# Attention and a mixture of experts on one core: when eight side jobs load, compute and store the sums of w2

## The chip, the cores and the metric

The kernel runs on 1 core of a Trainium2 chip. The metric is the device time of one execution in microseconds (us); lower is better. Below, PE is the matmul engine, DVE the vector engine, ACT the scalar engine, POOL the GpSimd engine, and SP the engine whose queue issues most of the DMAs.

## The reference

Per batch and head, attention over 576 positions goes through 32 memory slots. The result x (4608 rows of 512) then goes through four experts, each a two-layer perceptron with a hidden width of 1024, weighted by `p`:

```
a = softmax(phi, axis=2);  k_m = einsum('bhsm,bhsd->bhmd', a, k);  v_m = likewise with v
attn = softmax(q @ k_m.T / 8);  x = attn @ v_m          # (8, 8, 576, 64) -> (4608, 512)
p = domain_probs / sum(domain_probs)
for e in range(4):
    h = maximum(x @ w1[e], 0)                            # 4608 x 1024
    out += p[:, e:e+1] * (h @ w2[e])
```

All matmuls carry a value as two parts, a rounded high part and the remainder ("low"), and take three products (high by high, high by low, low by high). So every operand has to be split before it is used: ACT copies the high part, and DVE or POOL subtracts it (`split`, lines 156 and 157).

## The kernel before, in words

**Stages and steps.** The batches go in four pairs. The first two pairs take 2 x 128 = 256 numbered steps (`PAIR` = 128 steps for a pair, 32 for an expert: two batches, two row halves, eight blocks `j` of the hidden width). In step s the order of the program is: `accumulate` (L702, the results of a finished expert pass; for the last expert also the store L705), then `run_plan(s)`, then `first(s + 2)`, then `second(s)`. `first` makes the hidden activations of step s + 2 on PE (L647 to L649), ACT writes their high part (L659) and DVE their low part (L661, tile `h`). `second` multiplies them with w2 (L680 to L682; L682 is the product that needs the low part). PE therefore runs about two steps behind DVE. From step 36 on, nothing is rescheduled: each engine works through its own queue in just this order, so an instruction that waits holds up all that stands behind it on its engine. The two later pairs (`unit`, L1008 and others) use a scheme of products that needs sums of blocks of w2.

**The plan.** All side work hangs on steps, by tables of numbers written by hand: `at(s, unit)` puts a unit into step s, and `run_plan(s)` emits what was put there, in the order of putting. The units that matter here:

- Eight jobs `sums(s, own, e, fh)` (lines 195 to 238), one for each expert `e` and half `fh`, in the order of `JOBS`. A job loads two raw tiles of w2 on SP (L208, 512 KB each), makes four in-place sums on DVE (L231 to L234, two per step), then four times copies a high part on ACT (L220) and subtracts it on POOL (L221), and stores the results to memory by four DMAs that POOL issues (L226, 512 KB each). With `own` true its raw tiles lie in the one buffer `a` and the high parts in `tl` and `ph`, buffers that the attention of later batches uses as well; otherwise they take a buffer of `AT` (three) and two of `kvs` (three). So the next job with `own` can load only after the last one's stores have landed.
- `four` (lines 575 to 618): for the steps that use it, POOL splits a raw w1 tile in step s (L157), PE multiplies it in step s + 2 (L585, first with the high part, then with the low), ACT and DVE write the result into a `kvs` buffer (`vst`, L590 and L591), and POOL issues its store one step later (L573). These run from steps 70 and 230 on, one split in each step.
- `load_w2` (L193) and `load_vw` (L624) on SP fetch weights back, eight DMAs in a group; the program gives SP's DMAs eight landing semaphores in turn, so each of them waits until the one eight places ahead has landed.
- `units_w2` (L157 on POOL) splits w2 tiles in steps 61 to 68 and 93 to 100; `keep_w2` (L184 on POOL) stores split tiles.

The later pairs read the stored sums only from line 856 on, long after the jobs.

Of the kernel before, what the change touches and what calls it, by code (L numbers as in the profile page):

```python
# [28 lines left out]
PAIR = E * STEPS  # L29
# [40 lines left out]
UNITS = (NG - SEVEN) * E * 2 * 4  # L70
Q = 256
X_BANK, Y_BANK, AB_BANK = 4, 2, 6
JOBS = (62, 87, 99, 108, 117, PAIR + 28, PAIR + 85, PAIR + 94)
KEEP_AT, W2_AGAIN = 20, 24
FOUR_AT_7 = ((0, 4, 8, 12), (16, 20, 24, 28))
VW_LOAD_7 = ((21, 37), (26, 41))
# [4 lines left out]
def body(ctx: ExitStack, tc: tile.TileContext, qm, qt, kv, kvt, phi, prob, w1, w1d, w2, out):  # L81
# [105 lines left out]
    def keep_w2(e, j):  # L187
        leave(("w2", e, j), w2t[0, e, j])
        leave_now()
# [6 lines left out]
    def sums(s, own, e, fh):  # L196

        kept = []
        top, low = slice(0, Q), slice(Q, DM)
        sub, v = nc.vector.tensor_sub, nc.vector  # L200

        def load():
            tag = {"tag": "a"} if own else {"tag": "AT", "bufs": 3}
            t = att.tile([P, 2, 2, DM], F32R, name="raw", **tag)
            kept.extend(t[:, i].bitcast(F32) for i in range(2))
            kept.append(t)
            for i in range(2):
                nc.sync.dma_start(kept[i], w2[e, 2 * fh + i])  # L208

        def high(i, j):  # L210
            if j == 0:
                if own and i:
                    t = att.tile([P, 2, 640], F32R, name="sv", tag="ph")
                    t = t.rearrange("p a c -> p (a c)")[:, :2 * DM].rearrange("p (a c) -> p a c", a=2)
                elif own:
                    t = att.tile([P, 2, DM], F32R, name="sv", tag="tl")
                else:
                    t = att.tile([P, 2, DM], F32R, name="sv", tag="kvs", bufs=KVS)
                kept.append(t)
            nc.scalar.copy(kept[3 + i][:, j], kept[i][:, j])  # L220
            nc.gpsimd.tensor_sub(kept[2][:, i, j], kept[i][:, j], kept[3 + i][:, j].bitcast(F32))  # L221

        def store(i):
            d = dram.tile([P, 2, 2, DM], F32, name=f"v{e}{fh}{i}")
            for r, src in enumerate((kept[3 + i], kept[2][:, i])):
                nc.gpsimd.dma_start(d[:, :, r], src.bitcast(F32))  # L226
            for j in range(2):
                kept_for["v", e, fh, 2 * i + j] = d[:, j]

        at(s, load)  # L230
        at(s + 3, lambda: v.tensor_add(kept[1][:, :, low], kept[0][:, :, low], kept[1][:, :, low]))  # L231
        at(s + 3, lambda: sub(kept[0][:, :, low], kept[0][:, :, top], kept[0][:, :, low]))
        at(s + 4, lambda: sub(kept[0][:, :, top], kept[1][:, :, low], kept[0][:, :, top]))
        at(s + 4, lambda: sub(kept[1][:, :, top], kept[1][:, :, top], kept[0][:, :, top]))  # L234
        for i in range(2):
            for j in range(2):
                at(s + 4 + 2 * i + j, lambda i=i, j=j: high(i, j))
            at(s + 6 + 2 * i, lambda i=i: store(i))

    def units_w1(e, fh, g):  # L240
        kept = []
# [468 lines left out]
    def at(s, unit):  # L710
        plan[s].append(unit if isinstance(unit, tuple) else (None, unit))
# [76 lines left out]
    for k in range(NG):  # L788
        for e in range(E):
            s = k * PAIR + e * STEPS  # L790
# [34 lines left out]
    for e in range(E):  # L825
        for j in range(NJ):
            at(e * STEPS + KEEP_AT + j, lambda a=(e, j): keep_w2(*a))
    for n, s in enumerate(JOBS):
        sums(s, s != PAIR + 28, n // 2, n % 2)
    for s in FIRST_LOADS:  # L830
        at(s, lambda: load_part(wp.tile([P, 2, DM], F32R, name="w2", tag="w2", bufs=NJ + 1)))

# [447 lines left out]
```

## Time and profile before

| what | value |
|---|---|
| three timed runs | 1411.23, 1411.86, 1415.82 us; median 1411.86 |
| the profiled execution | 1409.54 us, its span 1407.4 us |
| granted PE clock | 0.994 on average |
| DMA over the span | 301.37 MB, 214 GB/s |
| loads of the jobs (L208) | 16, from 234.1 to 708.7 us, 3.8 to 12.0 us to land |
| stores of the jobs (L226) | 32, from 256.0 to 728.2 us |

The profile comes from one execution. Its times count from the first instruction. A line of it names an engine, a line of the kernel, what is written and read, and in brackets the idle time of that engine just before, with what ended it. A step is dated by the first L680 of its `second`: steps 72, 122, 227 and 230 begin at 262.40, 407.27, 708.34 and 727.20 us.

### The profile page before, as it was taken

Reading aid. Unit: us, or ns where it says so; the run is one execution under the profiler, and the core shown is the slowest. Engines: PE = TensorE matmul, PEld = TensorE weight load, DVE = VectorE, ACT = ScalarE, POOL = GpSimd, SP = SyncE. Lnnn points to the kernel's source line nnn. Section 1 sums busy time; section 2 is a strip of 40 time slices with the busy share of each in tenths; the row PEclk is TensorE's granted clock in tenths of the full one; section 3 lists DMA queues with packets and bytes.
Section 4 is the critical chain, followed back from the end, with each engine's and each line's share of the span. In section 5 each row is a group of like instructions: output and inputs, shape, how many; then the busy total and the mean of one; then the engine's idle time right before and its main releaser. Section 6 shows DMA issues by size and latency. Waiting matters only on the chain.

```text
span 1407.4 us, 25235 instructions
## 1 busy us (share of the span) xinstructions
PE 1366.8 (97%) x8894; PEld 1250.2 (89%) x8894; DVE 837.9 (60%) x1894; ACT 624.8 (44%) x1536; POOL 621.4 (44%) x660
## 2 busy tenths in 40 slices
PE   7899999999999999999979999999999999999998
PEld 6688888888878888889868999899999999999998
DVE  7775545446754365354434467777667666666665
ACT  7654555433444364463225354555543333333332
POOL 4410344755552334422245276676763334333333
PEclk9999999999999999999989999999999999999999
DMA  7832327799684264444588898999985776666662
GB/s 252 272 104 84 123 85 246 228 354 318 226 313 163 90 226 145 139 140 124 188 272 292 278 311 289 314 315 331 321 306 154 223 190 179 177 180 177 178 177 80
DMA packets 102029, 301.37 MB, mean 214 GB/s; under 512 B 24976, under 2 KB 26128, under 8 KB 101904
## 3 DMA queue, kind: packets, MB, share of 16 engines
q1 hardware_dynamic: 81168, 224.26, 51.3%
q0 software_dynamic: 20736, 75.51, 13.8%
q8 instruction: 71, 1.16, 0.4%
q14 instruction: 54, 0.44, 0.1%
HBM read 213.46 MB, written 84.93 MB: 212 GB/s over the span
## 4 chain that ended last, share of the span: by engine, by line
PE 58%; DMA 1%; DVE 1%; ACT 0%; issue 0%; POOL 0%; SPq 0%; DVEq 0%; ACTq 0%
PE banks L1008 22%; PE banks L922 5%; PE banks L923 5%; PE banks L924 5%; PE banks L682 3%; PE banks L680 3%; PE banks L681 3%; PE banks L585 2%; PE banks L647 2%; PE banks L648 2%; PE banks L649 2%; PE banks L1046 1%; PE banks L1047 1%; PE banks L1048 1%; PE banks L469 1%; PE banks L363 1%
## 5 line engine op out<-in xcount | busy, mean ns | idle before, releaser
L1026 DVE SCALAR_TENSOR_TENSOR acc<-banks,pt,acc 128x256 f32<-128x256 f32 x416 | 200.0, 481 | 108.9 <-PE banks L1008 105.2
L157 POOL TENSOR_TENSOR w<-stage,w 128x512 fp32r<-128x512 f32 x134 | 176.6, 1323 | 166.0 <-ACT w L156 153.9
L682 PE MATMUL banks<-w,h 128*128 128x512 f32 x512 | 201.9, 395 | 14.3 <-DVE h L661 14.3
L661 DVE SCALAR_TENSOR_TENSOR h<-banks,h 128x256 fp32r<-128x256 f32 x256 | 107.6, 420 | 164.3 <-ACT h L659 101.6
L680 PE MATMUL banks<-w,h 128*128 128x512 f32 x512 | 202.2, 395 | 1.7 <-DVE acc L702 1.3
L681 PE MATMUL banks<-w,h 128*128 128x512 f32 x512 | 201.7, 394 | 0.0
L659 ACT ACTIVATE h<-banks 128x256 fp32r<-128x256 f32 x256 | 97.8, 384 | 193.1 <-PE banks L649 152.2
L647 PE MATMUL banks<-AT,vw 128*128 128x256 f32 (+1 forms) x512 | 157.4, 308 | 5.7 <-ACT kvs L351 2.2
L1008 PE MATMUL banks<-w,a 128*128 128x256 f32 x1080 | 154.6, 282 | 0.3 <-DVE acc L1026 0.2
L648 PE MATMUL banks<-AT,vw 128*128 128x256 f32 (+1 forms) x512 | 151.7, 297 | 0.0
L922 PE MATMUL banks<-AT,vw 128*128 128x256 f32 (+1 forms) x512 | 151.6, 296 | 0.0
L649 PE MATMUL banks<-AT,vw 128*128 128x256 f32 (+1 forms) x512 | 151.2, 296 | 0.1
L923 PE MATMUL banks<-AT,vw 128*128 128x256 f32 (+1 forms) x512 | 151.1, 295 | 0.0
L924 PE MATMUL banks<-AT,vw 128*128 128x256 f32 (+1 forms) x512 | 150.9, 295 | 0.0
L1008 PEld LDWEIGHTS banks<-w,a 128*128 128x128 f32 x1080 | 143.6, 188 | 4.9 <-issue 0.9
L989 POOL TENSOR_TENSOR vt<-ph,vt 128x512 fp32r<-128x512 f32 x64 | 84.1, 1314 | 107.3 <-ACT vt L988 78.3
L682 PEld LDWEIGHTS banks<-w,h 128*128 128x128 f32 x512 | 96.5, 189 | 37.4 <-DVE h L661 16.0
L352 POOL TENSOR_TENSOR kvs<-stage,kvs 128x512 fp32r<-128x512 f32 x58 | 75.8, 1325 | 101.4 <-ACT kvs L351 100.9
L647 PEld LDWEIGHTS banks<-AT,vw 128*128 128x128 f32 x512 | 97.1, 190 | 18.0 <-DVE vw L562 4.0
L680 PEld LDWEIGHTS banks<-w,h 128*128 128x128 f32 x512 | 96.6, 189 | 13.7 <-DVE acc L702 1.8
L681 PEld LDWEIGHTS banks<-w,h 128*128 128x128 f32 x512 | 96.6, 189 | 11.0
L156 ACT CAST w<-stage 128x512 fp32r<-128x512 f32 x168 | 102.7, 619 | 6.3 <-DMA stage<-in_w 4.1
(149 smaller groups left out, 2985.6 us busy)
## 6 DMA issues: line engine op xcount, KB each, us to landing
w<-kw SPq DMA_DIRECT2D x93, 512.0 KB, 5.3
vwd<-vst POOLq DMA_DIRECT2D x80, 512.0 KB, 6.2
vw<-vwd SPq DMA_DIRECT2D x320, 128.0 KB, 5.7
w<-v SPq DMA_DIRECT2D x55, 512.0 KB, 5.5
stage<-in_w SPq DMA_DIRECT2D x44, 512.0 KB, 4.3
stage<-in_w1d SPq DMA_DIRECT2D x40, 512.0 KB, 4.7
stage<-in_kv SPq DMA_DIRECT2D x32, 512.0 KB, 3.9
kw<-w POOLq DMA_DIRECT2D x32, 512.0 KB, 6.7
```

The source lines that it names most:

```text
L157: eng.tensor_sub(dst[:, 1, :], raw, dst[:, 0, :].bitcast(F32))
L647: nc.tensor.matmul(ps, w[:, 0, f], at_t[:, g, 0, c], start=g == 0, stop=False)
L648: nc.tensor.matmul(ps, w[:, 0, f], at_t[:, g, 1, c], start=False, stop=False)
L649: nc.tensor.matmul(ps, w[:, 1, f], at_t[:, g, 0, c], start=False, stop=g == 1)
L680: nc.tensor.matmul(po[t], x[:, 0, :], w[:, 0, :], start=j == 0, stop=False)
L681: nc.tensor.matmul(po[t], x[:, 0, :], w[:, 1, :], start=False, stop=False)
L682: nc.tensor.matmul(po[t], x[:, 1, :], w[:, 0, :], start=False, stop=j == NJ - 1)
L922: nc.tensor.matmul(ps, w[:, 0, f], at_t[:, g, 0, c], start=g == 0, stop=False)
L923: nc.tensor.matmul(ps, w[:, 0, f], at_t[:, g, 1, c], start=False, stop=False)
L924: nc.tensor.matmul(ps, w[:, 1, f], at_t[:, g, 0, c], start=False, stop=g == 1)
L1008: nc.tensor.matmul(ps, a[:, l, jj], w[:, r, c], start=start and jj + i == 0, stop=jj == 1 and i == 2, skip_group_check=True,)
L1026: VE.scalar_tensor_tensor(a, src, p, a, ALU.mult, ALU.add)
```

## The change

The sums of a job come five and six steps after its load instead of three and four, and the later parts of the job move by the same two steps. The eight jobs start at other steps, and the one after step 128 that uses the shared buffers is joined by the first one. In order of the job:

| job (e, fh) | load before | load after | first sums before | first sums after |
|---|---|---|---|---|
| 1 (0, 0) | 62, own | 60, shared | 65 | 65 |
| 2 (0, 1) | 87 | 62 | 90 | 67 |
| 3 (1, 0) | 99 | 87 | 102 | 92 |
| 4 (1, 1) | 108 | 99 | 111 | 104 |
| 5 (2, 0) | 117 | 111 | 120 | 116 |
| 6 (2, 1) | 156, shared | 152, shared | 159 | 157 |
| 7 (3, 0) | 213 | 213 | 216 | 218 |
| 8 (3, 1) | 222 | 225 | 225 | 230 |

```diff
-JOBS = (62, 87, 99, 108, 117, PAIR + 28, PAIR + 85, PAIR + 94)
+JOBS = (60, 62, 87, 99, 111, PAIR + 24, PAIR + 85, PAIR + 97)
...
-        at(s + 3, lambda: v.tensor_add(kept[1][:, :, low], kept[0][:, :, low], kept[1][:, :, low]))
-        at(s + 3, lambda: sub(kept[0][:, :, low], kept[0][:, :, top], kept[0][:, :, low]))
-        at(s + 4, lambda: sub(kept[0][:, :, top], kept[1][:, :, low], kept[0][:, :, top]))
-        at(s + 4, lambda: sub(kept[1][:, :, top], kept[1][:, :, top], kept[0][:, :, top]))
+        at(s + 5, lambda: v.tensor_add(kept[1][:, :, low], kept[0][:, :, low], kept[1][:, :, low]))
+        at(s + 5, lambda: sub(kept[0][:, :, low], kept[0][:, :, top], kept[0][:, :, low]))
+        at(s + 6, lambda: sub(kept[0][:, :, top], kept[1][:, :, low], kept[0][:, :, top]))
+        at(s + 6, lambda: sub(kept[1][:, :, top], kept[1][:, :, top], kept[0][:, :, top]))
         for i in range(2):
             for j in range(2):
-                at(s + 4 + 2 * i + j, lambda i=i, j=j: high(i, j))
-            at(s + 6 + 2 * i, lambda i=i: store(i))
+                at(s + 6 + 2 * i + j, lambda i=i, j=j: high(i, j))
+            at(s + 8 + 2 * i, lambda i=i: store(i))
...
-        sums(s, s != PAIR + 28, n // 2, n % 2)
+        sums(s, s not in (60, PAIR + 24), n // 2, n % 2)
```

What this does to POOL's queue around steps 68 to 72, before. `raw_2441` and its `sv` tiles are those of job 1, `w2` is a split for the second expert layer, and `w1_2649` and `w1_2672` are the splits for the first two `four` multiplications:

```order
L157 TENSOR_TENSOR w2_2606<-stage_2398,w2_2606 128x512
L226 DMA v000_2609<-sv_2550 256x1x512
L226 DMA v000_2609<-raw_2441 256x1x512
L221 TENSOR_TENSOR raw_2441<-raw_2441,sv_2612 128x512 x2
L157 TENSOR_TENSOR w1_2649<-stage_2459,w1_2649 128x512
L226 DMA v001_2652<-sv_2612 256x1x512
L226 DMA v001_2652<-raw_2441 256x1x512
L157 TENSOR_TENSOR w1_2672<-stage_2459,w1_2672 128x512
```

The same place after. `raw_2383` is job 1, `raw_2444` job 2; the two splits for `four` are now `w1_2661` and `w1_2690`:

```order
L226 DMA v000_2614<-raw_2383 256x1x512
L221 TENSOR_TENSOR raw_2383<-raw_2383,sv_2617 128x512
L221 TENSOR_TENSOR raw_2444<-raw_2444,sv_2622 128x512
L221 TENSOR_TENSOR raw_2383<-raw_2383,sv_2617 128x512
L221 TENSOR_TENSOR raw_2444<-raw_2444,sv_2622 128x512
L157 TENSOR_TENSOR w1_2661<-stage_2462,w1_2661 128x512
L226 DMA v001_2664<-sv_2617 256x1x512
L226 DMA v001_2664<-raw_2383 256x1x512
L226 DMA v010_2667<-sv_2622 256x1x512
L226 DMA v010_2667<-raw_2444 256x1x512
L221 TENSOR_TENSOR raw_2444<-raw_2444,sv_2670 128x512
L157 TENSOR_TENSOR w1_2690<-stage_2462,w1_2690 128x512
```

Two subtractions of job 2 have come ahead of the first split, and two stores and one subtraction more ahead of the second.

SP's queue around the load of job 8 (`raw`), before. `w` is a tile of w2 (512 KB), `vw` a quarter tile (128 KB):

```order
L193 DMA w_6947<-kw_4088 128x1024
L193 DMA w_6967<-kw_4115 128x1024
L208 DMA raw<-in_w 128x1024 x2
L193 DMA w_6987<-kw_4150 128x1024
L624 DMA vw<-vwd_2950 32x1024
L624 DMA vw<-vwd_2980 32x1024
L624 DMA vw<-vwd_3012 32x1024
L624 DMA vw<-vwd_3052 32x1024
```

And after:

```order
L193 DMA w_6981<-kw_4161 128x1024
L624 DMA vw<-vwd_2973 32x1024
L624 DMA vw<-vwd_3003 32x1024
L624 DMA vw<-vwd_3035 32x1024
L624 DMA vw<-vwd_3075 32x1024
L624 DMA vw<-vwd_3109 32x1024
L624 DMA vw<-vwd_3141 32x1024
L624 DMA vw<-vwd_3168 32x1024
L624 DMA vw<-vwd_3201 32x1024
L208 DMA raw<-in_w 128x1024 x2
```

The two raw loads have moved behind one more tile of w2 and a whole group of eight `vw` loads.

## The prediction

> **What bounds the kernel now.** First the busy shares on the page, then PE's table of waits, then the view of the line that makes a job's first sum (L231), for what DVE waited for:
>
> ```profile
> PE 1366.8 (97%) x8894; PEld 1250.2 (89%) x8894; DVE 837.9 (60%) x1894; ACT 624.8 (44%) x1536; POOL 621.4 (44%) x660
> PE banks L682 <- DVE h L661: 14.3, 4, 9.9
>   DMA raw<-in_w: 19.5, 2
> ```
>
> PE is busy for all but 40.6 us of the 1407.4 us span, so the change can only win PE's waits, or add to them. Its largest wait is for the low part `h` of DVE, 14.3 us in 4 times; and DVE itself stood still for 19.5 us in two of the eight jobs because a raw tile had not landed. The timelines of DVE and PE show the two places (start, duration, ..., idle before with its releaser):
>
> ```profile
> 408.20 0.69 DVE L231 TENSOR_TENSOR raw<-raw 128x512 f32<-128x512 f32 x1 [5.55 <-DMA raw<-in_w]
> 410.01 0.50 PE L682 MATMUL banks<-w,h 128*128 128x512 f32 x1 [2.11 <-DVE h L661]
> 717.07 0.69 DVE L231 TENSOR_TENSOR raw<-raw 128x512 f32<-128x512 f32 x1 [13.94 <-DMA raw<-in_w]
> 718.87 0.79 PE L682 MATMUL banks<-w,h 128*128 128x512 f32 x1 [9.90 <-DVE h L661]
> ```
>
> Jobs 5 and 8 hold DVE; PE has about 4 us of lead and waits for the rest, 2.11 and 9.90 us. The second costs more than its gap. PE's timeline dates the steps by their first L680 (steps 226, 227, 228 and 230), and the table by windows has the granted clock (third value from the end):
>
> ```profile
> 706.25 0.40 PE L680 MATMUL banks<-w,h 128*128 128x512 f32 x1
> 708.34 0.40 PE L680 MATMUL banks<-w,h 128*128 128x512 f32 x1
> 722.02 0.63 PE L680 MATMUL banks<-w,h 128*128 128x512 f32 x1
> 727.20 0.40 PE L680 MATMUL banks<-w,h 128*128 128x512 f32 x1
> 712.00:716.00 4.00, 0.00 (x0) 0.00 (x0) 0.00 (x0) 0.00 (x0) 0.00 (x0) 0.69 1.03 412
> 716.00:720.00 4.00, 1.13 (x3) 0.94 (x4) 2.87 (x5) 0.51 (x1) 0.00 (x0) 0.50 1.05 248
> 720.00:724.00 4.00, 4.00 (x15) 3.38 (x14) 1.41 (x4) 2.58 (x7) 3.72 (x5) 0.53 0.65 201
> ```
>
> An undisturbed step takes 708.34 - 706.25 = 2.09 us. Steps 227 to 229 took 727.20 - 708.34 = 18.86 us, so the place costs 18.86 - 3 x 2.09 = 12.6 us: 9.9 of waiting, the rest at a clock of about 0.5. The most that the two waits hold is 2.1 + 12.6 = 14.7 us.
>
> **Job 5 (before at 117, now at 111).** SP's waits and its timeline:
>
> ```profile
> SPq L208 <- DMA v<-raw: 15.8, 2, 10.0
> 398.00 1.69 SPq L208 DMA_DIRECT2D raw<-in_w  x2
> ```
>
> Its load stood on SP until job 4's stores, planned in steps 114 and 116, had landed, which was in step 118 (396.8 to 399.6 us); the tiles came 10 us later, at 408.1. Now the stores are planned in 107 and 109: landed two steps later again, they free the load at its own step 111, and 10 us, under four steps of 2.8, end in step 115, ahead of the sums in 116. I take the whole 2.1 us as won. Should the landing take 3 us more, DVE's 4 us of lead cover it. Jobs 3, 4, 6 and 7 waited for nothing on DVE and get two steps more: nothing, with up to 1.5 us either way for transfers that meet others.
>
> **Job 8 (before at 222, now at 225).** SP's timeline, and two rows of its waits:
>
> ```profile
> 707.12 0.89 SPq L193 DMA_DIRECT2D w<-kw  x2
> 708.24 1.82 SPq L208 DMA_DIRECT2D raw<-in_w  x2
> 710.58 9.53 SPq L624 DMA_DIRECT2D vw<-vwd  x8
> SPq L624 <- DMA w<-kw: 7.0, 5, 2.5
> SPq L624 <- DMA raw<-in_w: 2.0, 2, 1.1
> ```
>
> The DMAs are full here (a share of 1.03 to 1.05 above), and SP runs some four steps behind the plan, each DMA waiting for the landing of an earlier one. So placing the load three steps later doesn't just move it in time: the raw tiles now go behind one `w` and eight `vw`, 0.52 + 1.05 = 1.57 MB. At 412 GB/s that is 3.8 us, at 330 (the mean of the first two windows) 4.8 us, so they land not at 717.0 but at about 721 (719 to 722.5, since job 7's stores, two steps later too, mix in differently). PE would want h of step 232 at 708.34 + 3 x 2.09 + 2 x 2.25 (the wider half, an estimate) + 0.5 = 719.6. From landing to PE took 718.87 - 717.0 = 1.9 us, so PE gets it at 722.9: a wait of 3.3 us is left.
>
> Then comes POOL. Job 8's subtractions now stand between the `four` splits of steps 232 to 236, whereas before they stood ahead of all of these. POOL's pitch is read from this stretch of its timeline, with the two PE rows that use the splits and the next step's L680s:
>
> ```profile
> 250.96 1.30 POOL L221 TENSOR_TENSOR raw<-raw,sv 128x512 fp32r<-128x512 f32 x1 [2.35 <-ACT sv L220]
> 252.21 1.30 POOL L157 TENSOR_TENSOR w<-stage,w 128x512 fp32r<-128x512 f32 x1
> 255.95 0.67 POOL L226 DMA_DIRECT2D v<-sv  x1
> 256.57 0.78 POOL L226 DMA_DIRECT2D v<-raw  x1
> 257.16 2.75 POOL L221 TENSOR_TENSOR raw<-raw,sv 128x512 fp32r<-128x512 f32 x2
> 259.64 1.49 POOL L157 TENSOR_TENSOR w<-stage,w 128x512 fp32r<-128x512 f32 x1
> 262.05 3.02 POOL L157 TENSOR_TENSOR w<-stage,w 128x512 fp32r<-128x512 f32 x2
> 261.19 0.50 PE L585 MATMUL banks<-w,vs 128*128 128x512 f32 x1 [0.86 <-POOL w L157]
> 262.40 0.40 PE L680 MATMUL banks<-w,h 128*128 128x512 f32 x1
> 263.79 0.63 PE L585 MATMUL banks<-w,vs 128*128 128x512 f32 x2
> 265.13 0.40 PE L680 MATMUL banks<-w,h 128*128 128x512 f32 x1
> ```
>
> A subtraction or split takes 1.25 us, a store's issue 0.6. From the sums' end (3.2 us after the landing) to the split of step 236 stand four L221, five L157, four L226 and four L573: 9 x 1.25 + 8 x 0.6 = 16 us. That is 721 + 19.5 = 740.5; PE, at 265.13 - 262.40 = 2.73 us a step with `four`, wants it 1.2 us ahead of step 238, at 719.1 + 6 x 2.73 - 1.2 = 734.3. So some 6.2 us of the 12.6 come back in pieces, and 6.4 us are won (4 to 9 over the landing's range).
>
> **Jobs 1 and 2 (now at 60 and 62).** Job 1's sums stay in step 65, so POOL still starts its first subtraction at 250.96. In the rows above it then never rests, and the first `four` already waits 0.86 us for it. Now two L221 of job 2 come ahead of the first split: 2.5 us. And job 2's sums meet a busy POOL, which before happened only rarely (POOL, DVE, POOL):
>
> ```profile
> 867.66 1.29 POOL L157 TENSOR_TENSOR w<-stage,w 128x512 fp32r<-128x512 f32 x1 [2.04 <-ACT w L156]
> 867.82 1.68 DVE L499 TENSOR_TENSOR at<-at,z 128x512 f32<-128x512 f32 x1
> 868.91 1.74 POOL L989 TENSOR_TENSOR vt<-ph,vt 128x512 fp32r<-128x512 f32 x1
> ```
>
> A DVE operation of two SBUF tiles and a POOL one don't run together: DVE's takes 1.68 instead of 0.69 and POOL's next 1.74 instead of 1.29, 0.45 more. Three such meetings add 1.35. The first split ends at 261.13 + 2.5 + 1.35 = 265.0, and PE is 3.8 us late. [...]
>
> Ahead of the second split stand four stores in a row now. POOL has issued a fourth store of a job only after the first of the four had landed:
>
> ```profile
> 694.91 0.92 POOL L226 DMA_DIRECT2D v<-sv  x1
> 698.12 0.69 POOL L226 DMA_DIRECT2D v<-raw  x1 [2.29 <-issue]
> 426.02 0.69 POOL L226 DMA_DIRECT2D v<-raw  x1 [3.82 <-DMA v<-sv]
> v<-sv POOLq DMA_DIRECT2D x16, 512.0 KB, 4.3
> DMA to landing us min/median/max: 3.0/4.9/11.3
> ```
>
> The first goes at 264.75; landing takes 3.0 at least and 4.3 in the median of v<-sv; the DMAs are not full at 266, so I take 3.5. The fourth is issued at 268.25, the subtraction follows 0.6 later, the split 1.25 after that and lasts 1.5: 271.6. Before, PE used it at 264.02 (the second of the pair at 263.79) without waiting. So PE is 7.6 us late in all. [...] Later splits come at less than a step's work and add nothing. DVE's delayed sums cost PE under 2 us at steps 69 and 70, which this larger wait swallows.
>
> **The sum**, against the profiled execution: 1409.54 - 2.1 - 6.4 + 7.6 = 1408.6. Its time lies 2.3 us below the median of the runs shown, so on the runs' scale that is 1411.0, against 1411.86: no change that a measurement could tell, whose bound is about 0.3%, 4.2 us.
>
> **The rivals.** *Faster.* Job 8's tiles land by 717.7 and POOL gives nothing back (all 12.6 won), and jobs 1 and 2 cost 4.8: -2.1 - 12.6 + 4.8 = -9.9, 1402. For it: SP's queue loses the raws' own 1.05 MB ahead of `vw`. Against it: those bytes only change places in full DMAs. Half of that, 4.2 us, is enough to be seen. I give 0.27 to all such cases.
>
> *Slower.* One mechanism, POOL at jobs 1 and 2: a fourth store that waits for a landing of 8 us instead of 3.5, adding 4.5, and decides from 6.5 us on. PE then idles over 8 us in one piece and the clock falls to 0.5 as at 713, another 2.5 us: 1411.0 + 4.5 + 2.5 = 1418. For it, landings up to 11.3; against it, DMA queues that aren't full there. 0.13. [...]
>
> *The change doesn't do what it says.* Job 8's loads, queued last, land at 725 or later and DVE waits as long as before; 6.4 won becomes 2.5: 1415. 0.1, half of it beyond the bound.
>
> **How the numbers follow.** The forecast, its terms within their bounds, has 0.5, the faster rival 0.27, POOL's 0.13, job 8's 0.1. The low end is near the faster rival, the high end near POOL's: 1403 to 1417.5. Faster by over 0.3%: 0.27. Slower: 0.13 + 0.05 = 0.18. Within: 0.55.
>
> **What would show it.** Right: no wait of DVE for raw near job 5; L585 waiting 6 to 9 us in all for POOL's split near 260 to 272; a fourth L226 there with a gap; DVE waiting for raw at job 8 for 5 to 9 us with PE waiting 2 to 5 behind it, then short waits of L585 for POOL. Wrong: L585 without waits near 262, or job 8's L231 without one.

## The result, and the profile after

Over seven runs each, taken together, the changed kernel takes 1423.30 us in the median (1418.77 to 1426.04) and the kernel before 1412.34 us (1408.67 to 1416.47). The ratio is 1.0069, 95% interval 1.0046 to 1.0093: slower by 11 us between the medians, by 10 by the ratio. The forecast was 1411.0, its range ended at 1417.5.

The profiled execution of the changed kernel took 1425.06 us, its span is 1423.2 us. It lies at the upper end of its runs, and the profiled execution of before (1409.54 us) at the lower end of its own, so the two profiles are further apart than the medians. Its first row on the page, PE's busy time:

```profile
PE 1377.2 (97%) x8894; PEld 1257.0 (88%) x8894; DVE 846.0 (59%) x1894; ACT 625.3 (44%) x1536; POOL 623.4 (44%) x660
```

Of the 15.8 us by which the span has grown, 10.4 are busy time of PE (1366.8 before), with the same 8894 matmuls: more of them ran at half clock (granted clock 0.988 on average, 0.994 before). PE's table of waits after (us in total, times, the longest):

```profile
PE banks L585 <- POOL w L157: 7.2, 4, 3.6
PE banks L682 <- DVE h L661: 7.1, 5, 4.0
...
PE banks L585 <- DVE vst L591: 2.2, 1, 2.2
...
PE banks L680 <- ACT h L659: 2.1, 3, 1.3
...
PE banks L647 <- DVE h L661: 1.9, 1, 1.9
```

The one wait of 9.9 us for `h` is gone. In its place stand six of 1.3 to 4.0 us, for POOL's split, for `h`, for `vst` and for ACT.

Where the time went is read from the steps, dated by their first L680 as before. The table gives, for stretches of steps, how much longer the stretch took than in the profile of before; the last three columns are experiments told below (pair_alone, six_alone and late_alone). Stretches that are not listed differ by 0.1 us at most, except 255 to the end of the span (-0.1 to +1.8; the last section has the reason).

| steps | changed | jobs 1, 2 alone | job 6 alone | jobs 7, 8 alone |
|---|---|---|---|---|
| 0 to 8 | +1.66 | -0.47 | +0.62 | -0.57 |
| 64 to 80 (jobs 1, 2) | **+10.38** | **+9.45** | 0.00 | 0.00 |
| 80 to 104 | -0.65 | -3.15 | -0.56 | -0.88 |
| 120 to 128 (job 5) | **-2.84** | +1.09 | +1.25 | +1.22 |
| 152 to 176 (job 6) | **+4.06** | -0.35 | **+2.75** | -0.44 |
| 224 to 248 (jobs 7, 8) | **+2.26** | -0.12 | +0.77 | **-0.23** |

With the 1.0 us by which step 0 began later, the first column gives the 15.8. The head of the program (up to step 8) is the same in all kernels of this study, and differs by -1.1 to +2.4 us from profile to profile: that is no effect of the change. Steps 80 to 104 are not steady either: the eight kernels of this study that run as before up to step 104 differ from it there by -0.88 to +0.25 us.

**Jobs 1 and 2.** POOL's timeline around the first two splits for `four`, and the two matmuls of PE that wait for them:

```profile
266.12 1.49 POOL L157 TENSOR_TENSOR w<-stage,w 128x512 fp32r<-128x512 f32 x1
267.32 0.94 POOL L226 DMA_DIRECT2D v<-sv  x1
...
268.49 1.21 POOL L226 DMA_DIRECT2D v<-sv  x1
271.04 0.69 POOL L226 DMA_DIRECT2D v<-raw  x1 [1.34 <-issue]
271.62 1.40 POOL L221 TENSOR_TENSOR raw<-raw,sv 128x512 fp32r<-128x512 f32 x1
272.84 1.39 POOL L157 TENSOR_TENSOR w<-stage,w 128x512 fp32r<-128x512 f32 x1
...
267.66 0.50 PE L585 MATMUL banks<-w,vs 128*128 128x512 f32 x1 [3.03 <-POOL w L157]
274.29 0.79 PE L585 MATMUL banks<-w,vs 128*128 128x512 f32 x1 [3.63 <-POOL w L157]
```

The picture is the one that was forecast: POOL rests only ahead of the fourth of four stores in a row, for 1.34 us, and L585 waits 6.66 us in two pieces (0.86 us in all before).

**Job 5.** DVE's first sum starts without a wait, where it waited 5.55 us before:

```profile
403.78 1.09 DVE L231 TENSOR_TENSOR raw<-raw 128x512 f32<-128x512 f32 x1
```

**Job 6.** Two rows of DVE in steps 157 and 158 of the changed kernel (L274 belongs to the softmax of `phi`), ACT's rows behind them, and the two waits of PE that follow:

```profile
517.59 0.15 DVE L274 TENSOR_SCALAR nm<-nm 128x1 f32<-128x1 f32 x1
...
520.89 0.68 DVE L233 TENSOR_TENSOR raw<-raw 128x512 f32<-128x512 f32 x1
...
521.60 0.62 ACT L220 CAST sv<-raw 128x512 fp32r<-128x512 f32 x1 [2.63 <-DVE raw L233]
522.12 0.38 ACT L659 ACTIVATE h<-banks 128x256 fp32r<-128x256 f32 x1
...
527.50 0.50 PE L680 MATMUL banks<-w,h 128*128 128x512 f32 x1 [1.30 <-ACT h L659]
533.28 0.58 PE L647 MATMUL banks<-AT,vw 128*128 128x256 f32 x1 [1.94 <-DVE h L661]
```

The same piece of ACT's work before:

```profile
518.57 0.61 ACT L220 CAST sv<-raw 128x512 fp32r<-128x512 f32 x1
519.09 0.37 ACT L659 ACTIVATE h<-banks 128x256 fp32r<-128x256 f32 x1
```

ACT now stands 2.63 us at its first copy. That copy needs the sum of L233, and DVE reaches its sums only behind its part of the softmax of `phi`. ACT's high part of `h` stands behind the copy in ACT's queue. Before, the copies came after the softmax and ACT did not wait at them.

**Job 8.** The load on SP, the first sum on DVE, PE's wait for `h`, and, 25 us later, a wait of ACT for a `vst` buffer whose store had not landed, with PE's behind it:

```profile
732.04 0.83 SPq L208 DMA_DIRECT2D raw<-in_w  x2
...
737.27 0.69 DVE L231 TENSOR_TENSOR raw<-raw 128x512 f32<-128x512 f32 x1 [10.16 <-DMA raw<-in_w]
739.08 0.79 PE L682 MATMUL banks<-w,h 128*128 128x512 f32 x1 [3.97 <-DVE h L661]
...
763.44 0.59 ACT L590 CAST vst<-banks 128x512 fp32r<-128x512 f32 x1 [5.26 <-DMA vwd<-vst]
764.90 0.77 PE L585 MATMUL banks<-w,vs 128*128 128x512 f32 x1 [2.22 <-DVE vst L591]
```

The table by windows for these places. The windows are those of 3.41 us in which the clock is granted (last section); busy PE stands second, the granted clock third from the end:

```profile
734.18:737.59 3.41, 0.93 (x6) 0.49 (x4) 0.32 (x1) 0.00 (x0) 0.00 (x0) 1.00 0.96 378
737.59:741.00 3.41, 1.92 (x5) 1.53 (x6) 2.94 (x7) 1.17 (x4) 0.38 (x1) 0.50 0.03 13
741.00:744.42 3.42, 3.42 (x12) 2.99 (x11) 3.42 (x8) 3.42 (x10) 3.40 (x4) 0.50 0.42 153
...
764.90:768.31 3.41, 3.13 (x10) 2.42 (x11) 2.16 (x6) 2.50 (x7) 2.78 (x4) 0.50 0.53 215
768.31:771.72 3.41, 3.41 (x11) 2.83 (x10) 2.02 (x5) 0.54 (x3) 2.40 (x4) 0.50 0.69 272
```

At each of the two waits, 3.97 and 2.22 us, the clock is halved for 6.83 us, from inside the first wait and from the end of the second. Before, one wait of 9.90 us had 10.24 us at half clock (713.53 to 723.77 us), and the wait itself lasted until 718.87, through half of them.

### The profile page after: what moved, and what is told of

Read it like the earlier page. It is cut to its first block, busy times and chain, and to the rows that moved or that the text cites. A ratio compares the mean times of both kernels' runs of the same rounds, so it can differ in the third digit from the quotient of the medians.

```text
span 1423.2 us, 25232 instructions
## 1 busy us (share of the span) xinstructions
PE 1377.2 (97%) x8894; PEld 1257.0 (88%) x8894; DVE 846.0 (59%) x1894; ACT 625.3 (44%) x1536; POOL 623.4 (44%) x660
## 4 chain that ended last, share of the span: by engine, by line
PE 84%; DVE 6%; DMA 4%; ACT 2%; issue 2%; POOL 1%; SPq 0%; ACTq 0%; DVEq 0%; POOLq 0%
PE banks L1008 22%; PE banks L682 8%; PE banks L681 8%; PE banks L680 8%; PE banks L922 5%; PE banks L923 5%; PE banks L924 5%; PE banks L647 4%; PE banks L648 4%; PE banks L649 4%; PE banks L585 2%; PE banks L469 2%; PE banks L363 2%; DVE vw L562 1%; PE banks L1046 1%
## 5 line engine op out<-in xcount | busy, mean ns | idle before, releaser
L680 PE MATMUL banks<-w,h 128*128 128x512 f32 x512 | 203.9, 398 | 4.5 <-ACT h L659 2.1
L647 PEld LDWEIGHTS banks<-AT,vw 128*128 128x128 f32 x512 | 98.1, 192 | 19.5 <-DVE vw L562 4.7
L680 PEld LDWEIGHTS banks<-w,h 128*128 128x128 f32 x512 | 97.5, 190 | 17.4 <-ACT h L659 3.6
L648 PEld LDWEIGHTS banks<-AT,vw 128*128 128x128 f32 x512 | 98.4, 192 | 8.6 <-DVE AT L532 0.3
```

What stands on the lines that cost most here:

```text
L647: nc.tensor.matmul(ps, w[:, 0, f], at_t[:, g, 0, c], start=g == 0, stop=False)
L648: nc.tensor.matmul(ps, w[:, 0, f], at_t[:, g, 1, c], start=False, stop=False)
L680: nc.tensor.matmul(po[t], x[:, 0, :], w[:, 0, :], start=j == 0, stop=False)
```

## The experiments

In the edits a job is written as (step of the load, own buffers, steps from the load to the first sums), and where a fourth number stands, it is the steps from the load to the first copy on ACT and its subtraction on POOL (otherwise one more than the third); the stores move with these. All times and ratios are against runs of the kernel before on the same chip.

**pair_alone: jobs 1 and 2 as changed, the rest as before.**

```diff
-JOBS = (62, 87, 99, ...)                      # all three steps
+JOBS = ((60, False, 5), (62, True, 5), (99, True, 3), ...)
```

> Jobs 1 and 2 alone as changed (60 and 62, five steps), jobs 3 to 8 as before. My theory now: the pair costs what the changed kernel shows between steps 64 and 80, 10.4 us: 6.6 us more waiting of PE and some 3.4 us of work at half clock behind the second wait; so the run is 10 us over before and every other place is as before. Rival (the forecast): 7.6 us, the waits alone, and the rest of the 10.4 comes from elsewhere. Rival: the pair is harmless without the later jobs, under 2 us.

Measured: 1417.31 us, ratio 1.0051 (1.0031 to 1.0070), by the ratio 7.2 us over before; steps 64 to 80 take 9.45 us more. So the pair is by far the largest cost, and needs none of the other changes. In steps 80 to 104 it gives 3.15 us back, 1.75 of them in step 99, where before PE waits 1.67 us for a load of q (L469); that wait is gone in all five kernels with job 2 at step 62, a gain that the prediction did not list. At the start of step 73, behind the second split, the profile is 7.69 us late (29.23 us from step 64, against 21.54): just the 7.6 of the forecast (8.66 in the changed kernel, whose clock was halved from 273.38 us, in its second wait). The other 1.8 us come later, by step 80, in which POOL is still catching up (a wait of 0.60 us at L585 in step 77 among them).

**warm: the changed kernel, with 8 matmuls of the identity ahead of each of the first two pairs of L585.**

```diff
-        ps = bank("pm", 512)
+        ps = bank("pm", 512); [nc.tensor.matmul(ps[:, :P], ident, ident, start=True, stop=True) for _ in range(fill.pop(0) if fill else 0)]
```

> The changed kernel with 8 extra matmuls of the identity (result unused) on PE ahead of each of the first two L585 pairs, where PE waits 3.0 and 3.6 us for POOL. My theory: the extra 1.7 us each fit inside the waits, which end when they ended; the clock is not halved at 273 us; the 3.4 us of half speed go, so steps 64 to 80 take 7 us more than before instead of 10.4. Rival: the waits alone made the 10.4; then nothing is won, and up to 1 us is lost.

Measured: 1419.08 us, ratio 1.0062 (1.0040 to 1.0084); steps 64 to 80 take 9.73 us more than before. The windows of the changed kernel at and behind its second wait:

```profile
269.96:273.38 3.42, 0.69 (x4) 0.22 (x2) 0.34 (x2) 0.00 (x0) 2.35 (x3) 1.00 0.94 351
273.38:276.79 3.41, 2.50 (x8) 2.41 (x9) 0.69 (x1) 1.13 (x3) 3.41 (x4) 0.50 0.75 241
276.79:280.20 3.41, 3.41 (x10) 2.64 (x10) 0.56 (x2) 0.54 (x3) 3.41 (x5) 0.50 0.74 275
```

The window of the second wait in warm, and the one behind it:

```profile
268.52:271.94 3.42, 2.46 (x19) 2.07 (x18) 0.31 (x2) 0.00 (x0) 2.36 (x3) 1.00 0.95 353
271.94:275.35 3.41, 2.51 (x13) 2.25 (x14) 1.12 (x3) 1.50 (x4) 3.41 (x4) 1.00 0.74 246
```

The added matmuls kept PE busy for 1.95 us ahead of each pair. The clock did stay whole (1.00 in both windows, against 0.50 in two of the changed kernel), and yet only 0.65 us of the 10.38 went. My theory fell: 6.83 us at half clock cost under 1 us here. POOL sets the pace behind the wait (busy 3.41 of 3.41 us in both), and the faster PE waits for it a little later (0.60 us at L585 in step 77, which the changed kernel has not). What is left is POOL's work, which the next run moves.

**pair_pool_later: pair_alone, with job 2's subtractions and stores behind the `four` splits.**

```diff
-        (62, True, 5)
+        (62, True, 5, 26)
```

> The pair_alone kernel with job 2's subtractions and stores moved on to steps 88 to 92, behind the four splits; its load and its sums stay. My theory: the pair's 9.5 us in steps 64 to 80 are POOL's work ahead of the first four splits; without it they fall under 3 us (job 1's own stands there before the change too, and DVE's sums of two jobs cost some 1.6 us in steps 69 and 70). Rival: the late h of DVE in steps 69 and 70 carries on by itself; then 5 us or more stay.

Measured: 1415.86 us, ratio 1.0029 (1.0016 to 1.0042). Steps 64 to 80 take 1.40 us more than before, instead of 9.45. So job 2's work behind the sums is the cost, and DVE's sums alone are not. ACT's copies moved along with POOL's part in this run; that it is POOL's part shows in the rows above, where PE waits for POOL's splits and POOL hardly rests. PE's row there, and one that came in step 95:

```profile
265.12 0.50 PE L585 MATMUL banks<-w,vs 128*128 128x512 f32 x1 [0.58 <-POOL w L157]
...
336.18 2.31 PE L469 MATMUL banks<-kT,stage 128*128 128x64 f32 x16 [2.89 <-DMA stage<-in_qm]
```

The second row is a wait for a load of q that lasted 0.18 us before; steps 80 to 96 take 2.75 us more with it. Why that load is later here was not tried, and part of the 2.75 may be chance: the changed kernel and six_later (below) are the same program up to step 152, and differ by 2.07 us in steps 80 to 96.

**six_alone: job 6 alone as changed; six_later: the changed kernel with job 6's sums where they stood before.**

```diff
-JOBS = (..., PAIR + 28, ...)                  # six_alone, against before
+JOBS = (..., (PAIR + 24, False, 5), ...)
...
-        (PAIR + 24, False, 5)                 # six_later, against the changed kernel
+        (PAIR + 24, False, 7)
```

> The kernel before with job 6 alone as changed (PAIR + 24, five steps). Theory: job 6's sums in steps 157 and 158 meet the softmax of phi; steps 152 to 176 are 4 us longer than before, as in the changed kernel (0.7 + 4.4 - 1.0), and the run is 3 to 4 us over before. Rival: this needs the other jobs' changes (another phase of SP's queue); then nothing changes.

> The changed kernel with job 6's sums and all behind them two steps later, where they stood before; its load stays at PAIR + 24. My theory: the sums' place against the softmax of phi in steps 157 to 159 costs 3.4 us, so steps 160 to 176 are as before, and the run is 3.4 us under the changed kernel (some 7.5 us over before). Rival: the load's earlier place or chance costs it, and the 3.4 us stay.

Measured: six_alone 1414.34 us, ratio 1.0018 (1.0003 to 1.0032), steps 152 to 176 +2.75 us with the same two waits as in the changed kernel (1.31 and 1.95 us). six_later 1416.18 us, ratio 1.0041 (1.0023 to 1.0060), steps 152 to 176 within 0.14 us of before. The load stayed at its new step there, so it is the place of the sums beside the softmax, and nothing else. The 1.31 us between +4.06 and +2.75 lie in steps 161 and 162, where the clock of the changed kernel was halved for 3.41 us (from 532.79 us) and that of six_alone was not.

**late_alone: jobs 7 and 8 alone as changed.**

```diff
-JOBS = (..., PAIR + 85, PAIR + 94)
+JOBS = (..., (PAIR + 85, True, 5), (PAIR + 97, True, 5))
```

> Jobs 7 and 8 alone as changed (five steps, job 8 at PAIR + 97), jobs 1 to 6 as before. My theory now: steps 224 to 248 take 2 us more than before: PE's wait for h falls from 9.9 to 4 us but is followed by half clock for 6.8 us, and a second wait of some 2 us comes at step 239, where the stores of vst stand behind the four stores of job 8; so the run is within 4 us of before, rather above it. Rival (the forecast): 6.4 us won.

Measured: 1409.22 us, ratio 0.9986 (0.9973 to 0.9998); steps 224 to 248 take 0.23 us less than before. Steps 224 to 232 win 12.43 us, steps 232 to 248 lose 12.20. The rows of PE that lose it, and the row of ACT ahead of the second:

```profile
723.31 0.50 PE L682 MATMUL banks<-w,h 128*128 128x512 f32 x1 [3.67 <-DVE h L661]
...
748.69 0.47 PE L585 MATMUL banks<-w,vs 128*128 128x512 f32 x1 [1.84 <-DVE vst L591]
...
747.23 0.58 ACT L590 CAST vst<-banks 128x512 fp32r<-128x512 f32 x1 [4.74 <-DMA vwd<-vst]
```

Step 232 alone takes 8.42 us instead of 2.73 (5.69 more), steps 235 to 240 take 6.52 more.

**eight_pool_later: late_alone, with job 8's subtractions and stores behind the last `four` split. eight_stores_later: late_alone, with only the stores moved there.**

```diff
-        (PAIR + 97, True, 5)
+        (PAIR + 97, True, 5, 21)              # eight_pool_later
...
-            at(s + hi + 2 + 2 * i, lambda i=i: store(i))
+            at(s + hi + (18 if s == PAIR + 97 else 2) + 2 * i, lambda i=i: store(i))   # eight_stores_later
```

> The late_alone kernel with job 8's subtractions and stores moved on by 15 steps, behind the last four split (from PAIR + 118); its load stays at PAIR + 97 and its sums at PAIR + 102. My theory: the wait of some 3.7 us for the raw tiles at step 232 and its half clock stay (about 6 us with what is lost at half clock), the waits at steps 235 to 239 go: steps 224 to 248 are 6 us shorter than before, against 0.2 in late_alone. Rival: the waits at steps 235 to 239 come from elsewhere (the vst stores themselves, the transfers held up) and stay.

> The late_alone kernel with only job 8's four stores moved on by 16 steps (to PAIR + 121 and PAIR + 123); its subtractions stay between the four splits. In late_alone steps 235 to 240 took 6.5 us more than before. Theory of the stores: the vst stores land late because they stand in POOL's queue behind job 8's 2 MB, and their tiles come free late; then the wait for vst at step 239 goes and steps 235 to 240 are within 2 us of before. Theory of POOL's time (the forecast): the splits are late because of the subtractions; then 4 us or more of the 6.5 stay, and PE waits for the splits.

Measured: eight_pool_later 1405.41 us, ratio 0.9953 (0.9932 to 0.9974); in steps 235 to 240 nothing is lost any more, and in 232 and 233 7.5 us. eight_stores_later 1405.68 us, ratio 0.9948 (0.9932 to 0.9965); steps 235 to 240 lose 1.8 us. All waits of PE from step 232 to 240 in eight_stores_later:

```profile
725.35 0.80 PE L682 MATMUL banks<-w,h 128*128 128x512 f32 x1 [4.02 <-DVE h L661]
742.05 0.50 PE L585 MATMUL banks<-w,vs 128*128 128x512 f32 x1 [0.23 <-POOL w L157]
748.70 0.50 PE L585 MATMUL banks<-w,vs 128*128 128x512 f32 x1 [0.59 <-POOL w L157]
```

No wait for `vst` is left. So of the 6.5 us, 4.7 went with the stores, and 1.8 stay with the subtractions, which stay in place here. How the 4.7 divide between POOL's time in issuing them and the later landing of the `vst` stores behind them in its queue, these runs do not say.

**eight_sums_later: before, with job 8's sums eight steps behind its load.**

```diff
-        (PAIR + 94, True, 3)
+        (PAIR + 94, True, 8)
```

> The kernel before with one thing changed: job 8's sums come eight steps behind its load instead of three (PAIR + 102), with its subtractions and stores behind them as ever. Its load stays at PAIR + 94, so the tiles land at about 717 us. My theory: DVE waits for nothing and the 12.4 us of steps 224 to 232 are won; the subtractions and stores now lie between the four splits and cost PE what steps 235 to 239 of the late_alone kernel show, waits of 3.3 us and half clock worth 1 to 2: steps 224 to 248 are 7 to 8 us shorter than before. Rival: POOL and the stores of vst cost most of the 12 us by themselves; then under 4 us are won.

Measured: 1408.41 us, ratio 0.9970 (0.9957 to 0.9983). Steps 224 to 248 take 6.18 us less than before: 10.17 won up to step 232, 3.99 given back after it. A little less than expected at the front, since PE now waits 0.40 and 1.38 us for a tile of w2 in steps 229 and 231, which the long wait had covered.

**warm_eight: eight_pool_later with 9 matmuls of the identity at the start of step 232.** They stand in `second`, ahead of the first L680, in the same way as in warm.

> The eight_pool_later kernel with 9 extra matmuls of the identity (result overwritten) on PE at the start of step 232, where PE then waits for h because job 8's tiles are late. Theory: the half clock behind this wait costs about 3 us of the 7.5 that steps 232 to 240 lost there; with the extra matmuls the window is busy enough, the clock stays whole, and steps 232 to 240 are 4 to 5 us longer than before instead of 7.5. Rival: as with the pair, another engine sets the pace behind the wait, so the clock makes no difference and the 7.5 stay.

Measured: 1405.88 us, ratio 0.9957 (0.9938 to 0.9976). Steps 224 to 248 take 5.2 us less than before (eight_pool_later 5.0). The matmuls ran in the window ahead of the one that held the rest of the wait (1.19 us of busy PE), and the window behind that one was halved all the same, for 3.41 us instead of the 6.83 of eight_pool_later. So this run does not settle what the clock costs here. The other profiles say a little more: steps 232 to 234 lost 5.6 to 5.8 us where the clock was halved for 3.41 us (eight_stores_later, late_alone, warm), and 6.6 to 7.5 us where it was for 6.83 (six_later, the changed kernel, eight_pool_later). Two of them had almost the same wait, 4.02 us (eight_stores_later) and 3.99 us (six_later), and differ by 1.0 us.

**best: job 5's sums two steps later, job 8's sums and POOL work later. best2: jobs 2 to 5 spaced anew, job 8 loaded later. best3: job 8 alone, loaded later.**

```diff
-JOBS = (62, 87, 99, 108, 117, PAIR + 28, PAIR + 85, PAIR + 94)     # all three steps
+(117, True, 5), (PAIR + 94, True, 8, 24)                            # best: these two
...
+(85, True, 4), (95, True, 4), (105, True, 4), (115, True, 4), (PAIR + 102, True, 13, 16)   # best2: these
...
+(PAIR + 102, True, 13, 16)                                          # best3: this one
```

> The kernel before with job 5's sums two steps later (five behind its load at 117), and job 8 with its load at PAIR + 94 as before, its sums at PAIR + 102 and its subtractions and stores behind the last four split (from PAIR + 118). Jobs 1 to 4, 6 and 7 as before. My theory: job 5 wins 2 to 3 us, job 8 all of its 12.4: 14 us under before, about 1398. Rival: job 8's late stores delay phase two's loads or the opening of its tiles, and 3 us or more come back between steps 246 and 256 or after; or the sums of job 5 in step 122 delay the attention of batch 4.

> Jobs 2 to 5 at 85, 95, 105 and 115 with the sums four steps behind the load (job 1, 6, 7 as before); job 8 loaded at PAIR + 102, its sums at PAIR + 115, its subtractions and stores from PAIR + 118. Theory: job 5's load no longer stands on SP for job 4's stores, so the 2.1 us at step 122 (and half clock) go; job 8's load behind the loads of w and vw ends the waits of 1.1 and 1.7 us for w in steps 229 and 231 that the best kernel has: all 12.4 us of steps 224 to 232 and 2.1 to 3 of steps 120 to 128 are won, 15 us under before in the profile. Rival: the sums in new steps meet the softmax of batches 2 and 3 in steps 92 to 117 and cost 2 us or more there.

> The kernel before with job 8 alone moved: loaded at PAIR + 102, sums at PAIR + 115, subtractions and stores from PAIR + 118. Theory: steps 224 to 248 are 12.4 us shorter than before and nothing else changes; the run is 12 us under before. Rival: the later load meets the loads of vw and the first loads of phase two, and the sums at step 243 come late: 3 us or more are given back between steps 240 and 256.

Measured: best 1403.68 us, ratio 0.9942 (0.9923 to 0.9961). Job 8 wins 9.2 us in steps 224 to 248; job 5 wins nothing (steps 120 to 128 as before). DVE still waits there, since the load stands on SP as long as before:

```profile
410.71 0.69 DVE L231 TENSOR_TENSOR raw<-raw 128x512 f32<-128x512 f32 x1 [3.44 <-DMA raw<-in_w]
```

best2 1407.29 us, ratio 0.9970 (0.9954 to 0.9987). Job 5 is cured (-2.84 us in steps 120 to 128), but steps 80 to 120 take 11.1 us more. PE's largest wait and SP's two rows ahead of it:

```profile
325.33 1.81 SPq L142 DMA_DIRECT2D stage<-in_w  x2
336.76 0.80 SPq L208 DMA_DIRECT2D raw<-in_w  x2
...
348.05 1.11 PE L469 MATMUL banks<-kT,stage 128*64 128x64 f32 x8 [4.13 <-DMA stage<-in_qt]
```

SP's table of waits has what held it:

```profile
SPq L208 <- DMA v<-raw: 21.1, 3, 10.4
```

SP issues nothing from 327 to 337 us, until the stores of the job before have landed, and the load of q stands behind it: steps 99 and 100 lose 5.3 us. (Steps 95 and 96 lose 3.7 more at an earlier load of q, which this hold does not explain.) The softmax met the moved work too, in step 113, where 2.2 us more were lost. Its product on DVE (L499) took 5.11 us instead of 1.22 before, while POOL issued two stores of job 4 and made three operations back to back beside it, and PE waited for the result:

```profile
387.45 5.11 DVE L499 TENSOR_TENSOR at<-at,z 64x256 f32<-64x256 f32 x1
...
393.22 0.34 PE L520 MATMUL banks<-ident,at 64*128 64x64 f32 x2 [1.91 <-DVE AT L532]
```

So the rival held for these 2.2 us, and a larger part, 5.3 us, came through SP.

best3 1399.19 us, ratio 0.9905 (0.9883 to 0.9928): the shortest time here, by the ratio 13 us under before. Its rows of SP and DVE for job 8, and the only wait of PE between steps 224 and 248:

```profile
717.86 0.82 SPq L208 DMA_DIRECT2D raw<-in_w  x2
...
755.80 1.53 DVE L231 TENSOR_TENSOR raw<-raw 128x512 f32<-128x512 f32 x1
...
712.57 0.47 PE L680 MATMUL banks<-w,h 128*128 128x512 f32 x1 [0.91 <-DMA w<-kw]
```

The tiles are loaded when SP has nothing more urgent behind them, the sums come 38 us after the load was issued, and POOL's part lies behind the last `four` split. 11.1 of the 12.6 us that the prediction put on job 8's old place are won.

## Why the prediction was wrong

**Job 5** (forecast -2.1): right, -2.84 in the profile, and for the reason given. Job 4's stores had landed by 386.79 us, the load was issued at 386.94, in its own step 111, and DVE did not wait.

**Jobs 1 and 2** (forecast +7.6): the mechanism was right, step by step, and so was the lateness behind the second split (7.69 us alone). The 1.35 us for three meetings of DVE and POOL held: beside job 2's sums three operations of POOL took 1.74, 1.73 and 1.74 us (from 254.89, 256.59 and 258.27 us), and the one ahead of them 1.29. In the profile of before, DVE's sums and L499 at 128x512 took 0.89 to 1.68 us in the six cases in which an operation of POOL was running at their start, and 0.67 to 0.69 in all others. The landing taken as 3.5 us was 3.4. As for the DMAs at 266 us, which the prediction calls not full: their share in the changed kernel was 0.39 (266.55 to 269.96 us), in before 1.05 (266 to 270). The step "Later splits come at less than a step's work and add nothing" failed: 1.8 us were added by step 80, while POOL was still behind, and 0.9 more in the changed kernel, whose clock was halved there.

**Job 8** (forecast -6.4, measured +2.26, alone -0.23): the wait of PE for `h` was forecast at 3.3 us and measured at 3.67 to 4.38. That it came so near is partly luck, since both its ends were later than forecast: counted from the start of step 227, the tiles landed after 15.3 us in the changed kernel and 13.8 in late_alone (12.7 forecast), and PE came to its wait after 13.2 and 12.1 (11.3 forecast). The step that failed is "some 6.2 us of the 12.6 come back": 12.2 came back in late_alone. Two things were missing from it. It priced the wait and POOL's lateness as one, the later covering the earlier; they add up, 5.7 us in step 232 and 6.5 in steps 235 to 240. And it counted only POOL's time: 2.4 us for the issue of four stores. In the runs the stores cost 4.7. The trace has a route that the sum left out: the stores of `vst` stand in the same queue behind 2 MB, ACT has only three buffers to write into, and it waited 4.74 us for `vwd<-vst` (L590); with the stores moved, no wait for `vst` is left. The 2.5 us between the changed kernel and late_alone are no fixed price. warm and six_later have the same jobs 7 and 8, and took +0.24 and -0.63 us in steps 224 to 248. Four windows of the clock were halved there in the changed kernel, two in late_alone and warm, three in six_later; that is the most likely source, but it was not taken apart.

**Job 6** (forecast "nothing, with up to 1.5 us either way"): the step failed outright, +4.06, alone +2.75. The prediction looked at whether the tiles would have landed, not at what else ACT and DVE do in steps 157 and 158. The waiting ACT instruction has the high part of `h` queued behind it.

**The sum**: -2.84 + 10.38 + 4.06 + 2.26 = +13.9 in place of -0.9. The lesser stretches (-0.65) and the head (+2.66) make 15.9, against 15.8 in the spans. The three parts run alone and job 5's gain add to 9.1. Job 8 is the largest error, 8.7 us in this profile and 6.2 alone; then come job 6 and the pair. The clock was halved at waits of 3.63, 1.94, 3.97 and 2.22 us, for which the main sum had put nothing.

**The rivals.** The slower one named POOL at jobs 1 and 2, with a fourth store waiting for a landing of 8 us; it waited 1.34 us, so that mechanism did not occur. The side came out as in that rival, for other reasons. The rival on job 8 (the change does not do what it says) came nearest by its outcome, since the gain at this place was lost, but not by its mechanism: DVE waited 10.16 us, not the 13.94 of before, and PE 3.97 instead of 9.90; the loss came behind that wait. No run shows the 4.8 us that the faster rival takes for jobs 1 and 2: by the prediction's own terms the 7.6 us become 4.6 without the store wait (1.7) and the three meetings (1.35), and the runs showed 9.45 (pair_alone) and 10.38.

**The signs** named in the prediction were seen but for one (no wait at job 5, 6.66 us for splits, the gap at the fourth store, PE 3.97 us behind job 8's tiles; DVE's wait for these tiles, 10.16 us, lay outside the 5 to 9, with 8.70 in late_alone). The sum was wrong all the same: the signs covered only the places that had been priced.

## What to carry to other kernels

A wait that is removed by moving work is won only if every engine that the work passes has room at the new place: list for each moved instruction what stands behind it, stores and their queue included, and look for the softmax, the splits and the buffers that live there. Work with a distant reader should go to a stretch that is empty on all its engines, load, sums and stores alike; best3 moved one job so and won 13 us, where the change, which moved all eight, lost 11. Before counting half clock as a loss, see which engine sets the pace there: 6.83 us of it cost under 1 us where POOL did.

## What the runs showed of the hardware

**The granted clock changed on a grid of 3.41 us, and the window ahead of a halved one was not always idle.** Between the first steps and the program's end, every stretch at half clock in the profiles of before and of the changed kernel lasts 3.41, 6.83 or 10.24 us. The same wait of about 2.1 us in step 122, in the windows of the clock's grid, first in before:

```profile
406.33:409.74 3.41, 1.56 (x10) 1.08 (x8) 1.51 (x3) 0.00 (x0) 0.00 (x0) 1.00 1.03 405
409.74:413.16 3.42, 3.01 (x15) 2.31 (x16) 2.35 (x5) 2.51 (x6) 1.75 (x2) 1.00 1.07 413
```

And in late_alone:

```profile
406.51:409.92 3.41, 1.46 (x6) 1.24 (x7) 3.00 (x5) 0.83 (x3) 0.05 (x1) 1.00 1.05 404
409.92:413.34 3.42, 3.42 (x12) 2.55 (x11) 2.23 (x4) 3.35 (x8) 3.40 (x4) 0.50 1.02 375
```

With 1.56 us of busy PE in the window the clock stayed whole, with 1.46 us (43%) it was halved for the next, which costs 1.2 us in steps 120 to 128. The grid lies differently against the kernel from one profile to the next: job 1's first sum (L231) starts 0.9 us into a window in before (246.79 us), and right where one begins in the changed kernel (249.48 us). The busy share alone does not decide it: in the changed kernel a window with 1.96 us of busy PE (from 529.38 us) was followed by a halved one, and one with 1.49 us (from 263.14 us) by a whole one. At one place behind step 255, a window with 1.75 us of busy PE in before (from 880.78 us) was followed by a whole one, and one with 1.75 in pair_alone (from 887.00 us) by a halved one. That is where most of the +1.8 us at the end of pair_alone comes from. The prediction's main sum had left this price out; in the profile of before, the only one at hand, the wait of 2.11 us had not halved the clock (1.00 in both windows).

**POOL issued the fourth of four stores in a row only when the first had landed**, here too: of the four that began at 267.32 us (two of job 1, two of job 2) the first landed at 270.73, and the fourth was issued at 271.04. The three gaps of this kind in the profile of before end in the same way: landings at 332.28, 425.69 and 697.80 us, issues at 332.62, 426.02 and 698.12.
